# A streaming multiply-add on one core: loads and stores on separate queues, a split tail, and a scalar spread by a matmul

## The chip, the core and the metric

The kernel runs on one core of a Trainium2 chip. The core has compute engines (TensorE for matmuls, VectorE, called DVE in the profile, ScalarE or ACT, GpSimd or POOL) and a SyncE (SP) that mostly issues transfers. Data moves between the chip's large memory (HBM, the `in_..._dram` and `out_dram` names of the profile) and the on-chip memory, which has 128 partitions, by 16 DMA engines. A transfer is issued by an instruction in the queue of SP or of ACT; the profile calls these queues SPq and ACTq. The metric is device time in microseconds (us); lower is better.

## The reference

```python
B, S, D = 512, 32, 640
x, fx: bfloat16 (B, S, D)      # random normal * 0.05
alpha: bfloat16 (1)

def reference(x, fx, alpha):
    return x + alpha * fx
```

Each of the three big arrays has 512 x 32 x 640 = 10,485,760 elements of two bytes, 20.97 MB. Two are read, one is written: 62.92 MB in all. One multiply and one add are done for each element.

## The kernel before

Rows are spread over 128 partitions so that each partition has one contiguous run of 81,920 elements of each array. The run is cut into ten chunks of 8192 columns. A tile of a chunk is 128 x 8192 bfloat16, 2 MB, with 16 KB in each partition.

```python
    xv = xf.rearrange("(p n) d -> p (n d)", p=P)
    fxv = fxf.rearrange("(p n) d -> p (n d)", p=P)
    ov = of.rearrange("(p n) d -> p (n d)", p=P)

    CHUNK = 8192
    # [cut: halve CHUNK until it divides F = 81920; it does at once]
    consts = ctx.enter_context(tc.tile_pool(name="consts", bufs=1))
    io = ctx.enter_context(tc.tile_pool(name="io", bufs=3))

    alpha_bf = consts.tile([P, 1], alpha.dtype)
    nc.sync.dma_start(out=alpha_bf[:], in_=alpha.to_broadcast((P, 1)))   # L44
    alpha_f32 = consts.tile([P, 1], mybir.dt.float32)
    nc.vector.tensor_copy(out=alpha_f32[:], in_=alpha_bf[:])             # L46

    for ci in range(n_chunks):
        sl = slice(ci * CHUNK, (ci + 1) * CHUNK)
        x_t = io.tile([P, CHUNK], xf.dtype)
        fx_t = io.tile([P, CHUNK], fxf.dtype)
        nc.sync.dma_start(out=x_t[:], in_=xv[:, sl])                     # L52
        nc.scalar.dma_start(out=fx_t[:], in_=fxv[:, sl])                 # L53
        nc.vector.scalar_tensor_tensor(                                  # L54
            out=x_t[:],
            in0=fx_t[:],
            scalar=alpha_f32[:],
            in1=x_t[:],
            op0=mybir.AluOpType.mult,
            op1=mybir.AluOpType.add,
        )
        nc.sync.dma_start(out=ov[:, sl], in_=x_t[:])                     # L62
```

The pool `io` holds three tiles of each name: a fourth `x_t` waits until the first is free, which is when its store has landed, since the multiply-add writes its result into `x_t`. A fourth `fx_t` waits only until the multiply-add has read the first. Alpha is loaded into all 128 partitions by one transfer with a repeated source.

Of the kernel before, what the change touches and what calls it, by code (L numbers as in the profile page):

```python
# [1 line left out]

# [4 lines left out]


@with_exitstack  # L10
def kernel(
    ctx: ExitStack,
    tc: tile.TileContext,
    x: bass.AP,
    fx: bass.AP,
    alpha: bass.AP,
    out: bass.AP,
):
    nc = tc.nc
    P = nc.NUM_PARTITIONS  # L20

    xf = x.flatten_outer_dims()
    fxf = fx.flatten_outer_dims()
    of = out.flatten_outer_dims()
    N, D = xf.shape
    assert N % P == 0, (N, P)
    rows_per_part = N // P
    F = rows_per_part * D

    xv = xf.rearrange("(p n) d -> p (n d)", p=P)  # L30
    fxv = fxf.rearrange("(p n) d -> p (n d)", p=P)
    ov = of.rearrange("(p n) d -> p (n d)", p=P)

    CHUNK = 8192
    while F % CHUNK != 0:
        CHUNK //= 2
    assert CHUNK >= 64
    n_chunks = F // CHUNK

    consts = ctx.enter_context(tc.tile_pool(name="consts", bufs=1))  # L40
    io = ctx.enter_context(tc.tile_pool(name="io", bufs=3))

    alpha_bf = consts.tile([P, 1], alpha.dtype)
    nc.sync.dma_start(out=alpha_bf[:], in_=alpha.to_broadcast((P, 1)))  # L44
    alpha_f32 = consts.tile([P, 1], mybir.dt.float32)
    nc.vector.tensor_copy(out=alpha_f32[:], in_=alpha_bf[:])  # L46

    for ci in range(n_chunks):
        sl = slice(ci * CHUNK, (ci + 1) * CHUNK)
        x_t = io.tile([P, CHUNK], xf.dtype)  # L50
        fx_t = io.tile([P, CHUNK], fxf.dtype)
        nc.sync.dma_start(out=x_t[:], in_=xv[:, sl])  # L52
        nc.scalar.dma_start(out=fx_t[:], in_=fxv[:, sl])  # L53
        nc.vector.scalar_tensor_tensor(  # L54
            out=x_t[:],
            in0=fx_t[:],
            scalar=alpha_f32[:],
            in1=x_t[:],
            op0=mybir.AluOpType.mult,
            op1=mybir.AluOpType.add,  # L60
        )
        nc.sync.dma_start(out=ov[:, sl], in_=x_t[:])  # L62


# [1 line left out]
_INS = ['x', 'fx', 'alpha']  # L66
_OUTS = [((512, 32, 640), 'bfloat16')]


# [23 lines left out]
```

## Time and profile before

| | |
|---|---|
| time, median of 4 runs | 161.61 us (161.39 to 161.93) |
| span of the profiled execution | 159.9 us |
| DVE busy | 87.5 us, 55% |
| multiply-add of 128 x 8192, mean of 10 | 8750 ns |
| moved between the memories | 62.92 MB, mean 394 GB/s over the span |
| queue q1 (x loads, stores, alpha) | 41.94 MB |
| queue q10 (fx loads) | 20.97 MB |

The span is the time from the first to the last instruction of one profiled execution; the time is measured without the profile and includes a little more. The profile's page shows the span in 40 equal slices: a digit per engine for its busy share in tenths, and for the DMA engines also the rate in GB/s. The chain that ended last is followed back from the last instruction, at each step to whatever released it. The waits view lists which engine or queue waited for whom: total us, times, and the longest. The windows view gives the busy time and the transfer rate of any stretch of the span. Idle time of an engine that isn't the bound costs nothing.

### The profile page before, as it was taken

The page shows a single profiled execution, that of the slowest core. Times are in us where ns is not written, and L with a number is a line of the kernel's source. Part 1 is how long each engine was busy: PE and PEld are TensorE (multiplying, and loading weights), DVE is VectorE, ACT ScalarE, POOL GpSimd, SP SyncE. Part 2 cuts the span into 40 slices and gives each one's busy share as a digit, 9 for nine tenths or more (in the row PEclk, how much of TensorE's full clock was granted, in tenths as well). Part 3 has the DMA queues.
Part 4 walks back from the last instruction along what each step waited for, and adds up shares of the span by engine and source line. Part 5 has one row for each costly group of instructions (what it writes and reads, how often), then busy time and mean ns, then how long its engine had stood idle before and what let it go on. Part 6 is the DMA issues. An engine that isn't in the chain of part 4 may idle for free.

```text
span 159.9 us, 125 instructions
## 1 busy us (share of the span) xinstructions
DVE 87.5 (55%) x11; POOL 0.2 (0%) x4
## 2 busy tenths in 40 slices
DVE  0000079999980001997940089389306954979920
POOL 0000000000000000000000000000000000000000
DMA  6899999999999999998999999999999999999166
GB/s 197 336 361 430 439 422 439 430 422 435 426 443 422 439 426 426 430 422 291 430 431 422 332 451 426 430 443 410 451 402 385 430 430 443 410 389 398 66 262 262
DMA packets 4464, 62.92 MB, mean 394 GB/s; under 512 B 624, under 2 KB 624, under 8 KB 624
## 3 DMA queue, kind: packets, MB, share of 16 engines
q1 hardware_dynamic: 3024, 41.94, 61.8%
q10 hardware_dynamic: 1440, 20.97, 32.4%
HBM read 41.94 MB, written 20.97 MB: 394 GB/s over the span
## 4 chain that ended last, share of the span: by engine, by line
DMA 66%; DVE 27%; SPq 1%; issue 1%; DVEq 0%
DMA x_t<-in_x_dram 58%; DVE x_t L54 27%; DMA out_dram<-x_t 9%; SPq L62 1%; SPq L44 0%; DVEq L54 0%; SPq L52 0%
## 5 line engine op out<-in xcount | busy, mean ns | idle before, releaser
L54 DVE SCALAR_TENSOR_TENSOR x_t<-fx_t,alpha_f,x_t 128x8192 bf16<-128x8192 bf16 x10 | 87.3, 8750 | 53.9 <-DMA x_t<-in_x_dram 53.9
L46 DVE CAST alpha_f<-alpha_bf 128x1 f32<-128x1 bf16 x1 | 0.2, 154 | 11.3 <-DMA alpha_bf<-in_alpha_dram 11.3
L77 POOL MEMSET const-bfloat16-1.0<- 128x1 bf16 x1 | 0.1, 102 | 0.0
L77 POOL MEMSET const-uint8-127<- 128x1 uint8 x1 | 0.1, 102 | 0.0
L77 POOL MEMSET const-float32-0.0<- 128x1 f32 x1 | 0.1, 99 | 0.2 <-issue 0.2
L77 POOL MEMSET const-float32-1.0<- 128x1 f32 x1 | 0.1, 99 | 0.0
## 6 DMA issues: line engine op xcount, KB each, us to landing
fx_t<-in_fx_dram ACTq DMA_DIRECT2D x10, 2048.0 KB, 14.6
x_t<-in_x_dram SPq DMA_DIRECT2D x10, 2048.0 KB, 19.9
out_dram<-x_t SPq DMA_DIRECT2D x10, 2048.0 KB, 13.0
alpha_bf<-in_alpha_dram SPq DMA_DIRECT2D x1, 0.2 KB, 10.5
```

The costliest lines, as they stand in the source:

```text
L46: nc.vector.tensor_copy(out=alpha_f32[:], in_=alpha_bf[:])
L54: nc.vector.scalar_tensor_tensor(out=x_t[:], in0=fx_t[:], scalar=alpha_f32[:], in1=x_t[:], op0=mybir.AluOpType.mult, op1=mybir.AluOpType.add,)
L62: nc.sync.dma_start(out=ov[:, sl], in_=x_t[:])
L77: nc = _bacc.Bacc("TRN2", target_bir_lowering=False, num_devices=1)
```

## The change

The change reorganises how the stream is issued. Both loads of a chunk go to SP's queue, all stores and the load of alpha to ACT's. The result gets a tile of its own, from a pool of three, so that a load tile is free once the multiply-add has read it. The last 8192 columns are loaded as 4096, 2048 and 2048, and the last of these is computed and stored in parts of 1024, 512, 256 and 256 columns, so that the last steps are short. Alpha is loaded into one partition and spread to 128 by a matmul with a vector of ones.

```diff
+CHUNK = 8192
+MID = [4096, 2048]
+TAIL_SUB = [1024, 512, 256, 256]
+LD_BUFS = 3
+OUT_BUFS = 3
+DVE_FRAC = 1.0
+STORE_ENG = "scalar"
+LOADX_ENG = "sync"
+LOADFX_ENG = "sync"
+ALPHA_ENG = "scalar"
 ... [cut: the list of loads: nine of 8192, then 4096, 2048, and a tail of 2048]
-    io = ctx.enter_context(tc.tile_pool(name="io", bufs=3))
+    ld = ctx.enter_context(tc.tile_pool(name="ld", bufs=LD_BUFS))
+    outp = ctx.enter_context(tc.tile_pool(name="outp", bufs=OUT_BUFS))
+    tailp = ctx.enter_context(tc.tile_pool(name="tailp", bufs=1))
 
-    alpha_bf = consts.tile([P, 1], alpha.dtype)
-    nc.sync.dma_start(out=alpha_bf[:], in_=alpha.to_broadcast((P, 1)))
+    alpha_bf = consts.tile([1, 1], alpha.dtype)
+    alpha_eng.dma_start(out=alpha_bf[:], in_=alpha.to_broadcast((1, 1)))
+    ones = consts.tile([1, P], alpha.dtype)
+    nc.vector.memset(ones[:], 1.0)
+    alpha_ps = psum.tile([P, 1], mybir.dt.float32)
+    nc.tensor.matmul(alpha_ps[:], lhsT=ones[:], rhs=alpha_bf[:], start=True, stop=True)
     alpha_f32 = consts.tile([P, 1], mybir.dt.float32)
-    nc.vector.tensor_copy(out=alpha_f32[:], in_=alpha_bf[:])
+    nc.vector.tensor_copy(out=alpha_f32[:], in_=alpha_ps[:])
 ... [cut: compute() issues the same scalar_tensor_tensor as before on columns a to b,
 ...  with DVE_FRAC = 1.0 all of it on DVE, writing o_t; the old loop goes]
+    for ci, (o, c, kind) in enumerate(loads):
+        sl = slice(o, o + c)
+        if kind == "tail":
+            x_t = tailp.tile([P, c], xf.dtype, tag="tx", name="tx")
+            fx_t = tailp.tile([P, c], fxf.dtype, tag="tfx", name="tfx")
+            o_t = tailp.tile([P, c], of.dtype, tag="to", name="to")
+        else:
+            x_t = ld.tile([P, CHUNK], xf.dtype, tag="x", name="x_t")
+            fx_t = ld.tile([P, CHUNK], fxf.dtype, tag="fx", name="fx_t")
+            o_t = outp.tile([P, CHUNK], of.dtype, tag="o", name="o_t")
+        x_eng.dma_start(out=x_t[:, :c], in_=xv[:, sl])
+        fx_eng.dma_start(out=fx_t[:, :c], in_=fxv[:, sl])
+
+        if kind == "tail":
+            a = 0
+            for sc in tail_sub:
+                b = a + sc
+                compute(o_t, x_t, fx_t, a, b)
+                st_eng.dma_start(out=ov[:, o + a:o + b], in_=o_t[:, a:b])
+                a = b
+        else:
+            compute(o_t, x_t, fx_t, 0, c)
+            st_eng.dma_start(out=ov[:, sl], in_=o_t[:, :c])
```

## The prediction

> **What bounds the kernel now.** I read the page from the top: busy shares, the slices, the chain. VectorE (DVE) is busy 87.5 us of 159.9, and the slices show the DMA engines near full from the second slice on, then nearly idle at the very end.
>
> ```profile
> DVE 87.5 (55%) x11; POOL 0.2 (0%) x4
> ...
> DMA  6899999999999999998999999999999999999166
> GB/s 197 336 361 430 439 422 439 430 422 435 426 443 422 439 426 426 430 422 291 430 431 422 332 451 426 430 443 410 451 402 385 430 430 443 410 389 398 66 262 262
> DMA packets 4464, 62.92 MB, mean 394 GB/s; under 512 B 624, under 2 KB 624, under 8 KB 624
> ```
>
> So the mover of 62.92 MB is the bound, and only slices well under 430 can be won. The chain of work that ended last says the same: two thirds transfers, and 27% multiply-adds.
>
> ```profile
> DMA 66%; DVE 27%; SPq 1%; issue 1%; DVEq 0%
> ```
>
> I then had the windows view price the lost stretches. Columns: window, its length, DVE busy, POOL busy, TensorE clock, DMA share, GB/s.
>
> ```profile
> 0.00:12.00 12.00, 0.15 (x1) 0.20 (x4) 1.00 0.81 298
> 12.00:70.00 58.00, 32.82 (x4) 0.00 (x0) 1.00 1.01 431
> 70.00:142.00 72.00, 44.89 (x6) 0.00 (x0) 1.00 1.00 415
> 142.00:148.70 6.70, 5.64 (x2) 0.00 (x0) 1.00 0.85 359
> 148.70:152.70 4.00, 3.99 (x1) 0.00 (x0) 1.00 0.00 0
> 152.70:159.90 7.20, 0.00 (x0) 0.00 (x0) 1.00 0.69 291
> ```
>
> Take 431 GB/s, held for 58 us, as full rate. All bytes at that rate need 62.92 / 0.431 = 146.0 us. Each window loses length x (1 - rate/431): start 3.7, middle 2.7, then 1.1 + 4.0 + 2.3 = 7.4 at the end. These sum to 13.8, and 146.0 + 13.8 = 159.8, the span. This ledger is what the change can work on.
>
> The start: finer windows give 270 GB/s in 0 to 6 us, 279 in 6 to 10, 418 in 10 to 12. The dip in 6 to 10 costs 4.0 x (1 - 279/431) = 1.4 us. It lies just where alpha is under way: it is issued at 0.73 and takes 10.5 us for 0.2 KB.
>
> ```profile
> alpha_bf<-in_alpha_dram SPq DMA_DIRECT2D x1, 0.2 KB, 10.5
> ```
>
> The middle: the waits view of SyncE's (SP) queue shows loads held back behind stores. A load of x needs a tile whose previous result has been stored, since the result lies in the x tile; and stores stand in the same queue as those loads.
>
> ```profile
> SPq L62 <- DVE x_t L54: 125.2, 10, 21.3
> SPq L52 <- DMA out_dram<-x_t: 12.2, 4, 5.6
> ```
>
> The end: the timeline shows the last 8192-column multiply-add starting at 143.94, taking 8.75 us, while the store before it drains and nothing is left to move (0 GB/s from 148.7 to 152.7). Its own store is issued at 152.7, lands 6.3 us later, and the program ends 0.9 us after that.
>
> **What the Trainium skill says.** "HBM Reference", Specifications: a core streaming alone measures about 425 GB/s, bounded by its 16 DMA engines. The trace agrees: 431. "DMA: Bandwidth & Descriptors", Queues, rings and completion order: each DMA engine goes round-robin, a packet at a time, between the queues that have work. That explains how 128 two-byte pieces of alpha, between packets of fx, took 10.5 us. The same page, Why a DMA increments its semaphore by 16 and not by 1: a [1, 1] scalar runs on one engine; no run before shows such a transfer. "Perfetto Trace Analysis", DMA Optimizations, suggests one issuing engine for inputs and another for outputs, and splitting transfers so that some start sooner; it warns of overhead for small DMAs (under 2 KB). The trace before has only 16 KB rows and alpha's, so it can't say how the smaller rows here will do.
>
> **The change, part by part.**
>
> *Alpha.* Its 128 pieces become one piece, on ScalarE's (ACT) queue; a ones-vector matmul, a memset and a copy from PSUM spread it. The first two-tile load lands near 2 + 4.19/0.431 = 11.7 us, so these small instructions have 8 us or so of room, given a landing by 4 us: off the path. What it removes is the dip of 1.4 us. The first 3 us (0, 229, 147 GB/s in single microseconds) lose 2.1, and I keep those: start loss 2.1 + 0.1 = 2.2.
>
> *Loads on SP alone, stores on ACT, result in its own tile.* Loads then wait only for the multiply-add that read their tiles, not for a store. Is there always a load to move? A pair takes 9.7 us at full rate and a multiply-add 8.75, with three pairs of tiles. When a multiply-add ends, the next pair or the one after is still coming in, and the released tiles' loads join behind it. So SP should always have work. With stores also running, the two queues share about half and half, which slows loads, but the DMA engines stay full. The middle's 2.7 us should shrink; I keep 0.8 for uneven DMA engines and the smaller pieces.
>
> Also, x and fx of a chunk now come one after the other rather than side by side with three alike in front. The first multiply-add starts near 12 us, not 21.15. That alone gives no time where the mover is the bound, but stores begin 9 us earlier, so fewer remain at the end.
>
> *The tail.* The last 8192 columns become 4096, 2048, and 2048 computed and stored as 1024, 512, 256, 256. Call t the landing of the last full chunk. The mover has 4.19 MB of loads and, if earlier stores are done, 4.19 MB of stores left: 8.39 / 0.431 = 19.5 us. DVE has 8.75 for the full chunk and, at 8750/8192 = 1.07 ns a column, 4.4 + 2.2 + 1.1 + 0.55 + 0.27 + 0.27 = 8.8 for the rest; with 0.1 of overhead for each of six (an estimate below the 0.154 us of the one-column cast) 18.1. Then the last store: 6.3 - 2.10/0.431 = 1.4 us fixed, so 19.5 as well. DVE frees the full chunk's result at t + 8.75, the loads end at t + 9.7, and that store's start-up (under a microsecond) closes the gap. The two chains are level, so the engines move nearly to the end. What stays: from the last byte (158.05 before, by single-microsecond windows) to the end, 1.9 us, and 0.3 for the join. End loss 2.2, from 7.4.
>
> *Instructions.* Multiply-adds go from 10 to 15, DVE busy from 87.5 to about 88.3; the queues issue at 0.33 to 0.6 us each. Neither is near a bound.
>
> **Sum.** 146.0 + 2.2 + 0.8 + 2.2 = 151.2 us of span. The median time is 161.61 against a span of 159.9, 1.7 more; 151.2 + 1.7 = 152.9 us.
>
> **The rivals.**
>
> *One queue can't keep the engines full.* While no store runs, all loads now stand on one queue. Against it: from 139 to 142 us only the last x load is under way (fx landed at 127.4, the store before it at 139.1), and the rate is 437 GB/s.
>
> ```profile
> 139.00:142.00 3.00, 3.00 (x1) 0.00 (x0) 1.00 1.02 437
> ```
>
> Three microseconds are a thin basis. If a queue alone gave 400, and some 50 us ran so, the loss would be 50 x 31/431 = 3.6, giving 156.5.
>
> *Small rows cost.* The tail has rows of 8 KB down to 512 bytes. Alpha's 8 pieces on each engine cost 1.4 us in the ledger, 0.17 each. There are nine more transfers of 8 pieces; at that price all 72 would cost 12 us. I think alpha's two-byte pieces are special, since a 16 KB packet's mean time (61.8% x 159.9 x 16 / 2560 = 0.62 us) is nearly its bytes at full rate (0.61), which leaves no such surcharge visible; but cost hidden behind the bytes could emerge. A fifth of it is 2.4 us: 155.3.
>
> *The dip isn't alpha's.* If the engines are slow in their first 10 us whatever is loaded, 1.4 us stays: 154.3.
>
> *The end is another wait.* If loads fall behind stores in the sharing, the last full chunk lands late and the DVE chain, not the mover, sets the end. By the arithmetic above they are level, so this costs about a microsecond: 153.9.
>
> **Range and chances.** All rivals are losses on a gain of 8.7 us; two small ones together still give 155. Upside: if the middle loses nothing and the end joins cleanly, 152, and at the 437 of the short window the bytes need 2 us less. So 150.7 to 155.4. Crossing 158.4 (2% faster) would take the whole one-queue loss plus a small-row loss. Faster 0.96, same 0.03, slower 0.01.
>
> **What would show it.** After the change: alpha lands within 4 us and no dip remains in 6 to 10; the first multiply-add starts near 12; loads never wait for a store in SP's queue; GB/s at 425 or more through the middle; no window at zero near the end; under 2.5 us from the last byte to the end. Rates under 415 with only loads running would show the first rival; a drop in the last 10 us with DVE idle the second; DVE busy without a break while transfers pause, the fourth. The prediction fails if the full rate itself changes, for instance because reads and writes now overlap more often.

## The result, and the profile after

The changed kernel takes 152.96 us (median of 11 runs, 152.73 to 153.22) against 161.66 us for the kernel before, a ratio of 0.944 (95% interval 0.941 to 0.948; the ratios here leave out runs in which the whole program ran slower, and aren't quite the quotients of the medians). The prediction was 152.9, in 150.7 to 155.4.

First the page's busy shares and slices of the changed kernel, to set beside those of before.

```profile
span 151.4 us, 147 instructions
...
PE 0.2 (0%) x1; PEld 0.1 (0%) x1; DVE 88.4 (58%) x17; POOL 0.2 (0%) x4
...
DMA  5999999999999999999999999999999999999995
GB/s 186 433 415 433 437 441 342 420 433 437 441 420 424 437 446 420 420 433 450 428 420 433 437 441 420 420 433 450 424 420 433 437 437 433 403 413 421 438 409 201
DMA packets 5618, 62.92 MB, mean 415 GB/s; under 512 B 626, under 2 KB 1010, under 8 KB 1778
```

The same bytes move; the slow slices at the start (336, 361) and the nearly empty one at the end (66) are gone. One new low slice has come, the seventh (342). The chain that ended last is four fifths transfers:

```profile
DMA 78%; DVE 13%; DVEq 2%; SPq 1%; issue 1%
```

The windows view, in the columns window, length, PE, PEld, DVE and POOL busy, TensorE clock, DMA share, GB/s:

```profile
0.00:12.00 12.00, 0.16 (x1) 0.10 (x1) 0.32 (x2) 0.20 (x4) 1.00 0.87 351
12.00:70.00 58.00, 0.00 (x0) 0.00 (x0) 35.58 (x5) 0.00 (x0) 1.00 1.01 425
70.00:142.00 72.00, 0.00 (x0) 0.00 (x0) 48.50 (x7) 0.00 (x0) 1.00 1.01 429
142.00:151.40 9.40, 0.00 (x0) 0.00 (x0) 3.99 (x5) 0.00 (x0) 1.00 0.81 331
```

The prediction's ledger, length x (1 - rate/431), gives 2.2 us at the start, 0.8 + 0.3 in the middle and 2.2 at the end. With 146.0 for the bytes that is 151.5, against the 151.4 of the span.

| us lost to the full rate | start (to 12) | 12 to 70 | 70 to 142 | from 142 |
|---|---|---|---|---|
| before | 3.7 | 0.0 | 2.7 | 7.4 |
| predicted | 2.2 | 0.8 in both | | 2.2 |
| after | 2.2 | 0.8 | 0.3 | 2.2 |

The first multiply-add starts at 13.07 us instead of 21.15 (the prediction had it near 12), as the timeline of the changed kernel shows. The last transfer's bytes are all but moved by 149.9 (393 GB/s from 142, 7 GB/s from there to the end).

```profile
13.07 8.75 DVE L102 SCALAR_TENSOR_TENSOR o_t<-fx_t,alpha_f,x_t 128x8192 bf16<-128x8192 bf16 x1 [10.76 <-DMA fx_t<-in_fx_dram]
...
127.94 15.41 DVE L102 SCALAR_TENSOR_TENSOR o_t<-fx_t,alpha_f,x_t 128x8192 bf16<-128x8192 bf16 x3 [7.78 <-DMA fx_t<-in_fx_dram]
143.26 2.73 DVE L102 SCALAR_TENSOR_TENSOR to<-tfx,alpha_f,tx 128x1024 bf16<-128x1024 bf16 x4
144.57 2.54 ACTq L142 DMA_DIRECT2D out_dram<-to  x4
```

### The profile page after: what moved, and what is told of

The parts are those of the page before. It is cut to its first block, busy times and chain, and to the rows that moved or that the text cites. A ratio compares the mean times of both kernels' runs of the same rounds, so it can differ in the third digit from the quotient of the medians.

```text
span 151.4 us, 147 instructions
## 1 busy us (share of the span) xinstructions
PE 0.2 (0%) x1; PEld 0.1 (0%) x1; DVE 88.4 (58%) x17; POOL 0.2 (0%) x4
## 4 chain that ended last, share of the span: by engine, by line
DMA 78%; DVE 13%; DVEq 2%; SPq 1%; issue 1%
DMA fx_t<-in_fx_dram 48%; DMA out_dram<-o_t 18%; DMA tx<-in_x_dram 12%; DVE o_t L102 12%; DVE to L102 2%; DVEq L173 2%; SPq L134 1%; SPq L135 1%; DVEq L102 0%
## 5 line engine op out<-in xcount | busy, mean ns | idle before, releaser
L102 DVE SCALAR_TENSOR_TENSOR o_t<-fx_t,alpha_f,x_t 128x8192 bf16<-128x8192 bf16 (+2 forms) x11 | 85.4, 7780 | 55.6 <-DMA fx_t<-in_fx_dram 55.6
L102 DVE SCALAR_TENSOR_TENSOR to<-tfx,alpha_f,tx 128x256 bf16<-128x256 bf16 (+2 forms) x4 | 2.7, 743 | 0.0
```

The lines of the kernel that those rows point to most:

```text
L102: nc.vector.scalar_tensor_tensor(out=o_t[:, a:a + g], in0=fx_t[:, a:a + g], scalar=alpha_f32[:], in1=x_t[:, a:a + g], op0=ALU.mult, op1=AL ...
```

## The experiments

A good total can come from wrong parts. So each part was first done alone on the kernel before, or undone alone in the changed kernel. Medians in us; ratios are to the kernel before on the same chip.

| kernel | us | ratio, 95% interval |
|---|---|---|
| before + alpha in one piece | 160.97 | 0.996, 0.993 to 0.999 |
| before + queues | 160.28 | 0.993, 0.991 to 0.996 |
| before + queues + own result tile | 159.63 | 0.990, 0.987 to 0.993 |
| before + split tail | 157.54 | 0.973, 0.969 to 0.977 |
| changed, alpha in 128 pieces | 153.80 | 0.949, 0.945 to 0.954 |
| changed, result in the x tile | 153.40 | 0.951, 0.946 to 0.956 |
| changed, no split tail | 158.26 | 0.978, 0.973 to 0.983 |
| changed, old queues | 161.03 | 0.996, 0.994 to 0.997 |

### Alpha alone, on the kernel before

```diff
-    alpha_bf = consts.tile([P, 1], alpha.dtype)
-    nc.sync.dma_start(out=alpha_bf[:], in_=alpha.to_broadcast((P, 1)))
+    alpha_bf = consts.tile([1, 1], alpha.dtype)
+    nc.sync.dma_start(out=alpha_bf[:], in_=alpha.to_broadcast((1, 1)))
     # and ones, the matmul and the copy from PSUM, as in the change
```

> The kernel before with alpha loaded as one piece and spread by the matmul, nothing else changed. Theory (the dip from 6 to 10 us is alpha's): 1.4 us less, about 160.2 us; x of the first chunk lands near 12 us instead of 21, the rate from 6 to 10 us is above 400 GB/s. Rival (the engines are slow in their first 10 us whatever is loaded): 161.6 us, dip unchanged.

Measured: 160.97 us, 0.8 less. The windows view of this kernel:

```profile
6.00:10.00 4.00, 0.00 (x0) 0.00 (x0) 0.00 (x0) 0.00 (x0) 1.00 1.06 455
10.00:12.00 2.00, 0.00 (x0) 0.00 (x0) 0.00 (x0) 0.00 (x0) 1.00 0.94 401
```

455 GB/s from 6 to 10 us, where it was 279: the dip was alpha's. The start loses 2.2 instead of 3.7. The first multiply-add starts at 15.42 us, not near 12 as expected. The total gives less than the start does, and why is not shown: the 20 runs spread from 160.28 to 162.67 us, and the profiled one took 162.11, well above the median. In that run the middle loses 0.7 + 3.0 and the end 8.5, so there what is won at the start is given back. The shortest runs, 160.28 against 161.25 for the kernel before on this chip, differ by 1.0.

### The split tail alone, on the kernel before

```diff
-    for ci in range(n_chunks):
+    # loads: nine of 8192, then 4096, 2048, 2048; the last one in tiles of its own
+    for ci, (o, c) in enumerate(loads):
         ...                                  # in place, on the old queues
+        for sc in ([1024, 512, 256, 256] if last else [c]):
+            # multiply-add and store of sc columns
```

> The kernel before with the last 8192 columns split (loads of 4096, 2048, 2048; the last computed and stored as 1024, 512, 256, 256), in place and on the old queues. Theory (the 7.4 us of the end are mostly the last full multiply-add and its store, alone): about 5 us less, 156.5 us, no window at zero near the end. Rival (in the old queues the last loads wait for stores, so the split alone does little): 159 us or more.

Measured: 157.54 us, 4.2 less. The windows view:

```profile
70.00:142.00 72.00, 47.13 (x6) 0.00 (x0) 1.00 0.99 411
142.00:155.70 13.70, 8.01 (x3) 0.00 (x0) 1.00 0.88 355
```

The end loses 13.7 x (1 - 355/431) = 2.4 us instead of 7.4, what the theory asked. The stretch from 70 to 142 loses 3.3 instead of 2.7 and the one from 12 to 70 loses 0.3 instead of nothing (429 GB/s). Those 0.9 us given back are why the total misses the expected 156.5 by a microsecond. The last 2048 columns have tiles of their own here, so they are loaded from 30.37 on and computed at 47.19; only their stores come last, at 150.46. The multiply-adds that end this kernel are those of 4096 and 2048 columns.

### Queues alone, then with a tile for the result

```diff
-        nc.scalar.dma_start(out=fx_t[:], in_=fxv[:, sl])
+        nc.sync.dma_start(out=fx_t[:], in_=fxv[:, sl])
-        nc.sync.dma_start(out=ov[:, sl], in_=x_t[:])
+        nc.scalar.dma_start(out=ov[:, sl], in_=x_t[:])
```

> The kernel before with both loads on SP's queue and stores on ACT's (alpha stays on SP with 128 pieces), in place. Theory (the 2.7 us of the middle come from loads behind stores, through the tile as well as the queue): a part of it only, 160.0 to 161.6 us. Rival (the queue is the whole cause): 159.0 us or less. Rival (one queue for loads is too slow): over 162 us.

The second kernel has this edit and `o_t = outp.tile([P, CHUNK], of.dtype)` as the multiply-add's output and the store's source.

> The kernel before with loads on SP, stores on ACT and a result tile of its own from a pool of three; alpha and the tail as before. Theory: the middle's loss falls from 2.7 to about 1 us, 159.9 us. Rival (loads were never short of a tile, the middle's dips are something else): 161.6 us.

Measured: 160.28 and 159.63 us. The windows view of the first kernel, from 70 us on, and then the wait that its SP queue shows:

```profile
70.00:142.00 72.00, 43.56 (x5) 0.00 (x0) 1.00 1.01 431
142.00:158.50 16.50, 8.75 (x1) 0.00 (x0) 1.00 0.51 216
```

```profile
SPq L52 <- DMA out_dram<-x_t: 112.5, 7, 34.3
```

Loads of x are held for stores 112.5 us in all, since the result still lies in the x tile, and yet the rate from 70 us on is the full 431 (from 12 to 70 it is 425, a loss of 0.8). So the old loss of 2.7 us came from the shared queue and not from the shared tile; my theory named both. The kernel with the old queues and a result tile, further down, agrees: it moves 414 GB/s from 70 to 142, a loss of 2.8. The total of 160.28 lies in the theory's range all the same, because the end now loses 16.5 x (1 - 216/431) = 8.2. The result tile of the second kernel takes 0.7 off that end (7.5); its middle is the same, 425 and 431. Its 159.63 is close to the expected 159.9 by luck: the theory had the gain of the tile in the middle.

### The result in the x tile, in the changed kernel

```diff
-            o_t = outp.tile([P, CHUNK], of.dtype, tag="o", name="o_t")
+            o_t = x_t          # likewise in the tail
```

> The changed kernel with the result written into the x tile, so that a load of x waits for the store of three chunks before. Theory: the middle loses again, up to 1.7 us more, 153.5 to 154.7 us. Rival (the mover has enough queued either way): 153.0 us.

Measured: 153.40 us, 0.4 more, with intervals of the two ratios that overlap. Its rates are 425 and 429 in the two middle windows, as in the changed kernel, though its loads of x are held for stores 122.3 us in all. The rival's mechanism holds: a waiting load is not a waiting mover. The lower edge of the theory's range was not reached.

### Alpha in 128 pieces, in the changed kernel

```diff
-    alpha_bf = consts.tile([1, 1], alpha.dtype)
-    alpha_eng.dma_start(out=alpha_bf[:], in_=alpha.to_broadcast((1, 1)))
-    # ones, matmul, copy from PSUM
+    alpha_bf = consts.tile([P, 1], alpha.dtype)
+    alpha_eng.dma_start(out=alpha_bf[:], in_=alpha.to_broadcast((P, 1)))
```

> The changed kernel with alpha again loaded into 128 partitions by one transfer with a repeated source, on the ACT queue; no matmul. Theory: 1.4 us more, 154.4 us, with a dip in the first 12 us. Rival (not alpha's): 153.0 us, no difference.

Measured: 153.80 us, 0.8 more, between the two. The windows view:

```profile
0.00:12.00 12.00, 0.15 (x1) 0.20 (x4) 1.00 0.81 300
12.00:70.00 58.00, 35.79 (x5) 0.00 (x0) 1.00 1.00 430
```

The start loses 3.6 instead of 2.2, all of the expected 1.4. But from 12 to 70 this kernel has 430 GB/s where the changed kernel has 425, 0.7 us better. The low slice near 25 us is missing here. So the one-piece load is worth 1.4 us at the start, and a dip that the kernel with 128 pieces doesn't have takes half of it back.

### No split tail, in the changed kernel

```diff
-MID = [4096, 2048]
-TAIL_SUB = [1024, 512, 256, 256]
+MID = []
+TAIL_SUB = []
```

> The changed kernel with ten chunks of 8192 columns and no split tail. Theory: the mover idles while the last full multiply-add runs and its store is alone; end loss 6.3 to 7.5 us instead of 2.2, so 157.1 to 158.3 us. Rival (separate queues and an earlier first multiply-add are what shortened the end): below 155 us.

Measured: 158.26 us, 5.3 more. The slices of its page end as those of before did:

```profile
GB/s 188 419 440 423 427 440 335 452 419 440 427 427 440 419 448 414 452 419 431 431 423 448 410 452 419 444 423 427 440 419 448 414 452 419 427 435 352 0 268 268
```

An empty slice under the last multiply-add, then the last store alone. The end loses 14.5 x (1 - 203/431) = 7.7. The split tail is the part that brings the gain; early stores don't replace it.

### The old queues, in the changed kernel

```diff
-STORE_ENG = "scalar"
+STORE_ENG = "sync"
-LOADFX_ENG = "sync"
+LOADFX_ENG = "scalar"
```

> The changed kernel with x loads and stores on SP's queue and fx loads on ACT's, as before; own result tile, split tail and alpha's one piece stay. Theory (stores that wait for a multiply-add hold loads behind them in the same queue): 0.5 to 2 us more, 153.5 to 155 us. Rival (all queues share the same engines and work is always queued): 153.0 us.

Measured: 161.03 us, 8.1 more: theory and rival both miss by far. The whole gain is gone, with the split tail, the result tile and the one-piece alpha all in place. Its timeline says why:

```profile
24.78 0.46 ACTq L135 DMA_DIRECT2D tfx<-in_fx_dram  x1
...
34.16 23.41 SPq L147 DMA_DIRECT2D out_dram<-o_t  x3
...
57.66 3.75 SPq L134 DMA_DIRECT2D x_t<-in_x_dram  x3
83.01 26.08 DVE L102 SCALAR_TENSOR_TENSOR o_t<-fx_t,alpha_f,x_t 128x8192 bf16<-128x8192 bf16 x3 [25.81 <-DMA x_t<-in_x_dram]
...
138.09 15.41 DVE L102 SCALAR_TENSOR_TENSOR o_t<-fx_t,alpha_f,x_t 128x8192 bf16<-128x8192 bf16 x3 [15.65 <-DMA x_t<-in_x_dram]
```

The second multiply-add ended at 34.13 and freed an x tile, but in SP's queue the next x load stands behind three stores, each of which waits for a multiply-add. It goes out at 57.66, 23.5 us late. The fx queue doesn't wait: it loads even the tail's fx at 24.78, long before it is of use. The late x load then takes 25.3 us to land, behind stores in its own queue and beside fx loads of the other one. DVE sits idle for 25.8 us meanwhile, and again before 138.09, though the engines are busy (425 GB/s from 12 to 70 us, 414 from there to 142). The last full chunk comes so late that the short tail stands behind it with little left to move: 247 GB/s from 142 on, a loss of 7.4.

The old queues alone are not this dear. The kernel before with the split tail has them too, with the result in the x tile and alpha in 128 pieces, and takes 157.54 us, 3.5 less. From 74 to 132 us its SP queue issues a store and an x load by turns, where here three stores stand in a row. No run separates the result tile from alpha in this, so how much of the 8.1 us is due to the order that came with the result's own tile stays open.

To see whether it is the stores in the load's queue or the two load queues that do this, stores went to a third.

### Three queues

```diff
-STORE_ENG = "scalar"
+STORE_ENG = "gpsimd"
-LOADFX_ENG = "sync"
+LOADFX_ENG = "scalar"
```

> The changed kernel with x loads on SP's queue, fx loads on ACT's and stores on a third, GpSimd's (POOL). Theory (the 161 us of the old queues come from x loads standing behind stores that wait for multiply-adds, in one queue; it matters that stores stand apart, not that both loads share a queue): 152.5 to 154.5 us. Rival (x and fx on two queues drift apart whatever the stores do): over 157 us.

Measured: 153.49 us (ratio 0.950, 0.947 to 0.952). Loads on two queues are as good as on one to half a microsecond once the stores stand apart. It too loads the tail early (x at 24.57, fx at 24.59), so early loads of the tail are not what costs.

### The fineness of the tail, and of the rows

```diff
-TAIL_SUB = [1024, 512, 256, 256]
+TAIL_SUB = [2048]
```

> The changed kernel with the last 2048 columns computed and stored in one piece. Theory (stores are still queued when the last multiply-add ends, so the mover sets the end): the same within 0.4 us of 153.0. Rival (the last small parts set the end, as the two level chains of the prediction have it): 1 us more, 154.0 us.

Measured: 153.04 us (ratio 0.947, 0.944 to 0.949), the same as the changed kernel. The timeline and the slices of this kernel:

```profile
142.69 2.34 DVE L102 SCALAR_TENSOR_TENSOR to<-tfx,alpha_f,tx 128x2048 bf16<-128x2048 bf16 x1
145.06 0.34 ACTq L142 DMA_DIRECT2D out_dram<-to  x1
```

```profile
GB/s 182 434 425 421 430 447 364 421 416 434 451 434 416 416 456 434 430 416 425 451 438 421 416 434 451 434 416 417 451 438 429 417 425 451 401 411 450 429 392 233
```

The last store goes out at 145.06. In the last slice but one (143.5 to 147.3) the engines still move 392 GB/s, most of it earlier stores, so they are busy when it comes, and four small parts in place of this one bring nothing measurable.

```diff
-CHUNK = 8192
-MID = [4096, 2048]
-TAIL_SUB = [1024, 512, 256, 256]
-LD_BUFS = 3
-OUT_BUFS = 3
+CHUNK = 4096
+MID = [2048]
+TAIL_SUB = [2048]
+LD_BUFS = 6
+OUT_BUFS = 6
```

> The changed kernel with chunks of 4096 columns (8 KB rows), six tiles of each name, and the last 4096 as 2048 and 2048 in one piece each. Theory (rows of 8 KB move as fast as rows of 16 KB, and the end is set by the mover): 152.5 to 153.5 us. Rival (more and smaller pieces cost): 155 us or more.

Measured: 154.28 us (ratio 0.954, 0.952 to 0.957), 1.3 more than the changed kernel and between the two. In the next kernel CHUNK is 1024, both pools hold 24 tiles, and MID and TAIL_SUB are empty.

> The changed kernel with 80 chunks of 1024 columns (2 KB rows), 24 tiles of each name and no special tail. 1920 pieces on each DMA engine instead of 240 in rows of 16 KB. Theory (a piece has a fixed cost of under 5 ns beside its bytes): under 162 us, DMA share near 1 throughout. Rival (20 ns or more of it, of the kind that alpha's pieces showed 170): over 185 us with DMA share near 1. If the share falls well below 1, the queues ran dry and the run says nothing of the pieces.

Measured: 183.74 us (ratio 1.133, 1.128 to 1.139), between the two. The windows view of this last kernel:

```profile
12.00:70.00 58.00, 0.00 (x0) 0.00 (x0) 34.25 (x27) 0.00 (x0) 1.00 1.02 364
70.00:142.00 72.00, 0.00 (x0) 0.00 (x0) 42.40 (x33) 0.00 (x0) 1.00 1.00 359
```

The DMA share is 1.0, so the queues didn't run dry; each piece takes longer. A 2 KB piece on one of 16 engines takes 2048 x 16 / 359 = 91 ns instead of 76 at 431 GB/s: 15 ns more, the completion of each transfer included. The same sum for rows of 8 KB (425 GB/s from 70 to 142, against 429) gives 3 ns. So the cost of small rows is real, but not a constant per piece, and far from the 170 ns of alpha's two-byte pieces.

No variant beats the changed kernel.

## Why the prediction was right, and where it wasn't

The predicted sum was 146.0 + 2.2 + 0.8 + 2.2 = 151.2 of span; measured 146.0 + 2.2 + 1.1 + 2.2 = 151.5. That the medians agree to 0.06 us is luck in part: the profiled run of the changed kernel took 153.22, the longest of the 11, and its sum is 0.3 above the predicted one. Point by point:

**The bound.** Right. The mover stays the bound, at the same full rate.

**Alpha.** Right in mechanism and size at the start: 1.4 us, gone with the 128 pieces and back with them. The one piece has landed when the matmul starts at 1.95. The alternation with fx packets, by which the prediction explained the 10.5 us of the 128 pieces, fits a run too: in the kernel before with the new queues fx loads stand behind alpha in SP's queue, and the cast that waits for alpha starts at 3.87 instead of 11.29. Its start loses 3.5 all the same (305 GB/s up to 12 us): the loads wait for alpha's pieces in the queue, and only 44 GB/s move in the first 3 us. In the total the one piece is worth 0.8 in the changed kernel, since a dip that the prediction didn't know of appears near 25 us.

**The first rival, one queue for all loads.** It fell. Up to 21.86 us only loads run, all from SP's queue, and from 12 to 22 the changed kernel moves 431 GB/s.

**The middle.** The size was nearly right (0.8 predicted, 1.1 measured), its content wrong. I kept 0.8 for uneven engines and small rows; most of what is left is the dip from 24 to 26 us, 2.0 x (1 - 270/431) = 0.7:

```profile
24.00:26.00 2.00, 0.00 (x0) 0.00 (x0) 2.00 (x1) 0.00 (x0) 1.00 0.92 270
```

I also put the old 2.7 us down to loads that wait for stored tiles. The runs put it down to the shared queue alone. And the sign I named, that loads never wait for a store in SP's queue, is wrong. The changed kernel's view of SP's waits has such waits still:

```profile
SPq L135 <- DMA out_dram<-o_t: 6.9, 3, 5.7
```

The tiles don't ask for them (the result has its own); what does is open. The longest cost nothing: from 31.62 to 37.69, when it ends, the rate is 432.

**What the queues are worth.** Understated. The prediction counted them into the 2.7 us of the middle. That fits the kernel before (1.2 us), but with the other parts in place the old queues cost 8.1: the prediction weighed loads behind stores only by the rate they had cost, not by what a late x load does to everything after it. The parts don't add: done alone, alpha, tail, and queues with tile bring 0.8 + 4.2 + 1.9 = 6.9 of the 8.7; undone alone, alpha, tile, tail and queues cost 0.8 + 0.4 + 5.3 + 8.1 = 14.6.

**The end.** Right in size, and the tail is the cause (5.3 us without it, 4.2 by itself on the kernel before). The two chains that the prediction held level were not: from the start of the last full chunk's multiply-add at 127.94, the multiply-adds end 18.1 us later as predicted, at 146.0, but the mover 22.0 later, at 149.9, instead of 19.5. It moved 9.0 MB at 410 GB/s there, where the sum had 8.39 MB at 431: the earlier stores weren't all done. So the mover set the end, and the fourth rival, that DVE would, fell. With about 3.9 us of transfers after the last multiply-add, its fineness should hardly matter, and it didn't.

**Small rows.** The rival's charge of 170 ns a piece was far too high, and so was its fifth, 34 ns; 2 KB rows cost 15. At that price the 72 added pieces would cost 1.1 us. What rows under 2 KB cost each was not measured; the run without them shows no gain.

## What to carry to other kernels

Price the stretches of a transfer-bound kernel against its own best sustained rate; the losses then say which stretch a change can win, and their sum checks itself against the span. Keep stores that wait for compute out of the queue that issues loads (worth 1.2 us in the kernel before and 8.1 in the changed one): a load behind such a store loses its turn even when its tile is free, and the other stream of a pair then fills the engines with data nobody can use yet. End on small chunks, but only until the mover, not the last instruction, sets the end.

## What the runs showed of the hardware that was not expected

In the changed kernel the rate falls to 270 GB/s for two microseconds, some 2 to 4 us after the first store is issued (21.86), with the DMA share still at 0.92. Kernels with loads on one queue and stores on ACT show it at the same distance: 295 GB/s from 25 to 27 in the kernel before with the new queues (first store at 23.24), 287 from 24 to 26 with the result in the x tile (21.87). With three queues it is there as well (295 from 27 to 29, first store at 24.48). With alpha's 128 pieces on ACT's queue, and first store at 23.48, it is absent: no two-microsecond window from 20 to 36 us is below 393. With the old queues it is weaker and later (344 from 28 to 30, first store at 24.39). In the changed kernel all 33 packets that start from 24 to 26 us belong to SP's loads; packets of ACT's store start only after 26. In the dips of the other three kernels named, too, all packets are of loads. So the dip comes just ahead of the first stored data, not beside it. A turn from reading alone to reading and writing that all engines make at once could look so, and so would its absence where alpha's pieces have put them out of step; no run here tests that, and the cause stays open.
